# Attention with routed experts: row maxima are split into two parts before their transpose, and shift rows and running-sum rows travel in fewer DMAs

## The chip, the cores and the metric

One core of one Trainium2 chip runs the whole program in one launch. The metric is the device time of that launch in microseconds (us), lower is better. A median over three executions is given for the kernel before. One further execution was recorded by the hardware profiler; all rows below come from that one.

## What is computed

The first half is a causal attention for 8 batches of 8 heads, 576 positions of width 64, with a bias made from running sums of a gate `s`. The second half sends each of the 4,608 resulting tokens through a group router, an expert router and one of 16 two-layer experts.

```
scores = scale * q @ k^T                         # scale = 1/8
cum    = cumsum(max(s, 0), axis=-1)
bias   = -(cum[:, :, :, None] - cum[:, :, None, :])
scores = where(causal, -1e9, scores + minimum(bias, 0))
attn   = exp(scores - max(scores)); attn /= sum(attn) + 1e-9
x      = (attn @ v)  as 4608 rows of 512
g, e   = argmax of softmax(x @ w_group), then of softmax(x @ w_expert[g])
out    = p_g * p_e * (relu(x @ w1[g, e]) @ w2[g, e])
```

## The kernel before

The attention works head by head; two heads are a pair, so there are 32 pairs and four pairs to a batch. A loop over `step` from -4 to 68 handles one head in three roles at once: role A (`rowmax`) finds the row maxima of the head four steps ahead, role B (`scores`) makes the transposed scores of the current head and their exponentials, and role C (`av`) multiplies the previous head's probabilities by v.

*Maxima.* For A, TensorE multiplies 66 rows of the operand tile `WA` (64 of q or k, and rows 64 and 65, which carry the running sums in two parts) into the PSUM tile `pm` (L214). VectorE adds the causal mask and takes the maximum over each row into a column of `mc`, a tile of 128 partitions by 10 columns (five row blocks of each head of the pair, L222). After the pair's last maximum, `shift_rows` transposes `mc` on TensorE into the PSUM tile `pmt` (L236), ten rows of 128. `shifts` then writes the negated maxima as a high part `th` (L242) and the remainder `tl` (L243), both read from PSUM, and `send` issues two DMAs on ScalarE's queue (L248): `th` into row 66 of `WA`, `tl` into row 67. Every operand of the scores travels as such a high and a low part.

*Scores.* For B, TensorE multiplies all 68 rows of `WA` (L269) and adds the product of the low parts in `WB` (L271) in the PSUM tile `ps`. Rows 66 and 67 subtract the maximum, so the exponential on ScalarE (L279) needs no bias. GpSimd zeroes the masked triangle with affine_select (L288).

*The rest of a pair.* C writes the PSUM tile `po` (L309), ScalarE copies values and sums out (`vals` L313, `sums` L316), VectorE transposes the sums, takes reciprocals and multiplies (`st`, `rc`, `xT`, L335 to L354). q and k of a later pair are split by `split`: the high parts `hl` on ScalarE (L152), the low parts on GpSimd with a tensor_tensor of 576 columns (L156), from which `load_a` and `load_b` fill `WA` and `WB` by DMAs on SyncE's queue. `load_a` also fetches the running-sum rows 64 and 65 of `WA`, one DMA per head (L179), for pairs 0 to 3 from the SBUF tile `cumh` and later from its copy `cumd` in DRAM, which is written at the end of step -1 (L571). A `Router` works per batch in pieces between the attention's instructions; it needs a few constants, which `Router.operands` makes with eight VectorE instructions in one go at the end of step -1 (L668 to L678).

*What sets the order.* TensorE, VectorE, ScalarE and GpSimd follow an order written out by hand in strings. In the string of an even step, `... B3 T C1 A3 B1 ...` stands for score unit 3, then `T` (the transpose of the maxima), a piece of C, a piece of A, score unit 1; `t` makes the two parts, `D` sends, `R` lets the router go one piece on, `a` takes one maximum. SyncE's order is left to a scheduler after step 0. The tiles `ps`, `pmt` and the odd `px` share three PSUM buffers of one pool, and which one a tile gets follows from the readers that release them. All DMAs share eight completion semaphores.

Of the kernel before, what the change touches and what calls it, by code (L numbers as in the profile page):

```python
# [8 lines left out]
F32 = mybir.dt.float32  # L9
F32R = mybir.dt.float32r  # L10
# [3 lines left out]
ALU = mybir.AluOpType  # L14
# [6 lines left out]
P = 128  # L21
# [5 lines left out]
QO = 64  # L27
QW = QO + S
KA, QA = 0, 1
# [25 lines left out]
def attn_moe(ctx, tc, qk, v, s, wr, w1, w2, out, stop_at=None, dbg=None):  # L55
# [22 lines left out]
    st.listed = {}  # L78

    attention(tc, qk, v, s, wr, xs, st)  # L80
    if dbg is not None:
        nc.sync.dma_start(dbg['x'], xs)
# [26 lines left out]
def attention(tc, qk, v, s, wr, xs, st):  # L109
    nc = tc.nc  # L110
    NP = B * H // 2
    LEAD = 4
    with ExitStack() as ctx:
# [4 lines left out]
        sm = ctx.enter_context(tc.tile_pool(name="sm", bufs=2))  # L118
# [8 lines left out]
        ident = st.ident  # L127
# [5 lines left out]
        WA = [wa.tile([68, 2, 2, QW], F32R, name=f"WA{i}") for i in range(NA)]  # L133
# [13 lines left out]
        def split(p, part, later=False):  # L147

            if part == 0:
                hls[p] = raw.tile([P, 3, S], F32R, name=f"hl{p}", tag="hl", bufs=3)  # L150
            hl, r = hls[p], raws[p]
            nc.scalar.copy(hl[:, part], r[:, part])  # L152

            def low(h):
                hr = slice(0, P) if part else slice(h * 64, h * 64 + 64)
                (nc.vector if p < 1 else nc.gpsimd).tensor_tensor(  # L156
                    out=hl[:, 2] if part else WB[p % NBB][0:64, KA, h], in0=r[hr, part],
                    in1=hl[hr, part].bitcast(F32), op=ALU.subtract)

            for h in range(1 if part else 2):  # L160
                if later:
                    push("G", p, lambda h=h: low(h))
                else:
                    low(h)
# [7 lines left out]
        def load_a(p, placed=False):  # L172
            w = WA[p % NA]
            hl = hls[p].bitcast(F32)
            for h in range(2):
                if h or not placed:
                    nc.sync.dma_start(w[0:64, :, h, QO:].bitcast(F32), hl[h * 64:h * 64 + 64, 0:2])
                n = 2 * p + h
                nc.sync.dma_start(w[64:66, KA, h, QO:].bitcast(F32), (cumh if p < 4 else cumd)[n:n + 1].bitcast(F32))  # L179

        def load_b(p, placed=False):
            w = WB[p % NBB].bitcast(F32)
# [49 lines left out]
        def shift_rows(p):  # L232
            need("a", 2 * p + 1)
            i = p % NA
            pt = ring(f"pmt{p}", "t", True)
            nc.tensor.transpose(pt[:10, :P], mc[p % 2], ident)  # L236
            push("t", p, lambda: shifts(p, i, pt))

        def shifts(p, i, pt):
            th = sm.tile([10, P], F32R, name=f"th{p}", tag="th", bufs=1)  # L240
            tl = sm.tile([10, P], F32R, name=f"tl{p}", tag="tl", bufs=1)
            nc.vector.tensor_scalar(out=th, in0=pt[:10, :P], scalar1=-1.0, scalar2=None, op0=ALU.mult)  # L242
            nc.vector.scalar_tensor_tensor(out=tl, in0=pt[:10, :P], scalar=-1.0, in1=th.bitcast(F32), op0=ALU.mult,  # L243
                                           op1=ALU.subtract)

            def send():
                for r, t in ((66, th), (67, tl)):
                    nc.scalar.dma_start(WA[i][r:r + 1, QA].bitcast(F32).rearrange("o h q -> o (h q)"), t.bitcast(F32))  # L248

            push("D", p, send)  # L250

# [165 lines left out]
        def push(k, i, f):  # L417
            fifo[k].append((i, f))

        def pop(k):  # L420
            if fifo[k]:
                i, f = fifo[k].pop(0)
                done[k].append(i)
                f()
# [6 lines left out]
        def need(k, i):  # L431

            while fifo[k] and fifo[k][0][0] <= i:
                pop(k)

        def ring(name, k="b", reader=False):

            kind, n = ringed[-3]
            while n >= len(done[kind]):
                pop(kind)  # L440
            ringed.append((k, len(done[k]) + len(fifo[k]) if reader else -1))
            return ps_s.tile([P, 512], F32, name=name, tag="ps")
# [12 lines left out]
        cumh = c0[:BH, 0:2 * S].rearrange("p (a s) -> p a s", a=2)  # L455
        s0, r1, c2 = (c1[:BH, i * S:(i + 1) * S].bitcast(F32) for i in range(3))
        cumd = dr.tile([BH, 2, S], F32, name="cumd")
# [26 lines left out]
        mc = [ac.tile([P, 10], F32, name=f"mc{i}") for i in range(2)]  # L484
# [6 lines left out]
        split(0, 0)  # L491
        split(0, 1)
        load_a(0, True)
        split(1, 0)
        split(1, 1)
        load_raw(2)
        place(0, 1)
        place(0, 2)
        place(1, 0)
        load_a(1, True)  # L500
        load_b(0, True)
        rt = Router(tc, ac, late, end, kept, ring, wr_f, wr_sb, xs, st)
# [8 lines left out]
        for t in VT:  # L511
            nc.gpsimd.memset(t[:, 0:NB, 2], 1.0)


        pre = {-2: [(load_a, 2, True), (load_raw, 3), (load_v, 0)],
               -1: [(load_b, 1, True), (load_raw, 4)],
               0: [(split, 3, 0), (split, 3, 1), (load_a, 3), (load_v, 1)],
# [15 lines left out]
        for step in range(-LEAD, NH + 5):  # L533
            m, a = step + LEAD, step - 1
            A = rowmax(m) if m < NH else []
            Bq, C = [], []
            if 0 <= step < NH:
                need("T", step // 2)
                need("t", step // 2)
                need("D", step // 2)  # L540
                pts[step] = PT[step % 2]
                Bq = scores(step, pts[step])
            if 0 <= a < NH:
                p = a // 2
                for k in "be":
                    need(k, a)
                if a % 2 == 0:
                    for k in "YZWK":
                        need(k, p - 2)
                    vals[p] = sm.tile([P, S], F32, name=f"vals{p}", tag="vals", bufs=2)  # L550
                    sums[p] = sm.tile([P, S], F32, name=f"sums{p}", tag="sums", bufs=2)
                C = av(a, pts.pop(a), vals[p], sums[p])
            if step >= 2 and step // 2 + 4 < NP:
                push("S", step // 2 + 4, lambda p=step // 2 + 4, part=step % 2: split(p, part, True))
            named = {"A": A, "B": Bq, "C": C}
            order = FIRST if step < 3 else ORDERS if step < NH - 1 else LAST
            for part in order[step % 2] if step > 0 else ORDER0:
                if part[0] in named:
                    for f in named[part[0]][int(part[1]):int(part[1]) + 1]:
                        f()  # L560
                elif part == "R":
                    rt.step(rt.done >= B - 2)
                elif part == "J":
                    if rt.done >= B - 2:
                        rt.step(True)
                else:
                    pop(part)
            for f, *args in pre.get(step, ()):
                f(*args)
            if step == -1:  # L570
                nc.sync.dma_start(cumd, cumh.bitcast(F32))  # L571
                rt.operands()
            if step == 62:
                manual.close()
                manual.enter_context(tc.manual_schedule(engines={ENG.PE}))
            if step == 0:
                manual.close()
                manual.enter_context(tc.manual_schedule(engines={ENG.PE, ENG.DVE, ENG.Activation, ENG.Pool}))
            if step % 2 == 1 and 0 < step < NH:
                for f, lead in ((load_a, 4), (load_b, 3), (load_v, 1), (load_raw, 6)):  # L580
                    if step // 2 + lead < NP and (f != load_v or step > 1):
                        need("S", step // 2 + lead)
                        if f in (load_b, load_raw):
                            need("G", step // 2 + lead - 2 * (f == load_raw))
                        f(step // 2 + lead)
# [39 lines left out]
class Router:  # L625
# [39 lines left out]
        ni = ac.tile([P, B, NB], I32, name="ni")  # L665
        self.n1, self.ni, self.uf, self.onesf = n1, ni, uf, onesf

    def operands(self):  # L668
        V, ni, n1 = self.tc.nc.vector, self.ni, self.n1
        V.tensor_copy(self.wr_sb[:, :, 0:20], self.wr_f)  # L670
        V.tensor_tensor(out=self.wr_sb[:, :, 32:52], in0=self.wr_f, in1=self.wr_sb[:, :, 0:20].bitcast(F32),
                        op=ALU.subtract)
        V.tensor_copy(self.ub, self.uf)
        V.tensor_copy(self.ob, self.onesf)
        V.tensor_scalar(out=ni, in0=n1, scalar1=6, scalar2=None, op0=ALU.arith_shift_right)
        V.tensor_copy(self.part[:, 0], ni)
        V.tensor_scalar(out=ni, in0=n1, scalar1=63, scalar2=None, op0=ALU.bitwise_and)
        V.tensor_copy(self.part[:, 1], ni)  # L678

    def step(self, now=False):  # L680

# [906 lines left out]
```

## Time and profile before

| | us |
|---|---|
| median of three executions | 945.64 (940.46 to 947.15) |
| profiled execution | 939.42 |
| its span in the trace | 937.7 |
| attention with its routing, in that span | about 0 to 440 |
| experts | about 440 to 938 |

How the views are read: the page gives each engine's busy time and, in 40 slices, the busy tenths and the TensorE clock that was granted. The table by stretches gives the same per window. The wait table of TensorE lists which instruction it waited for, with the total, the count and the longest wait. A timeline gives start and duration of each instruction, and in square brackets the idle time of that engine just before it and what released it. "PEld" is TensorE's weight load, "ACTq" the issue of a DMA by ScalarE.

### The profile page before, as it was taken

What the parts mean: (1) busy time and instruction counts of PE and PEld (TensorE: products, weight loads), DVE (VectorE), ACT (ScalarE), POOL (GpSimd) and SP (SyncE); (2) the same over time, 40 slices, a digit from 0 to 9 for tenths busy, and PEclk for the clock granted to TensorE, in tenths of its full rate; (3) what the DMA queues carried; (4) which work ended last, traced back from release to release, by engine and by line L of the source; (5) the groups of instructions that cost most, each with busy time, mean ns of one, the idle gap of its engine ahead of it and who ended that gap; (6) DMA issues with size and microseconds to landing.
All of it is one profiled execution on the core that took longest, in us unless ns stands there. A gap on an engine that the chain in (4) does not pass through costs nothing. (4 is left out here: it accounts for less than half of the span.)

```text
span 937.7 us, 17973 instructions
## 1 busy us (share of the span) xinstructions
PE 867.3 (92%) x5648; PEld 779.6 (83%) x5648; DVE 702.2 (75%) x2002; ACT 608.3 (65%) x1382; POOL 615.0 (66%) x732
## 2 busy tenths in 40 slices
PE   4889999999999999998887999999999999999993
PEld 3677788888878787886686999999999999999992
DVE  7546685877868685876487578998888899888830
ACT  5567677776777677767734556667676666766740
POOL 9656576665757576534875447666768778878750
PEclk9989999999999999999998999999999999999997
DMA  6999989888989889723646345455554556655510
GB/s 188 237 209 228 213 218 227 198 223 188 226 204 223 215 210 231 175 68 114 207 139 210 134 162 192 165 190 208 184 194 180 204 185 226 226 201 188 195 44 23
DMA packets 80502, 174.66 MB, mean 186 GB/s; under 512 B 9580, under 2 KB 42988, under 8 KB 72208
## 3 DMA queue, kind: packets, MB, share of 16 engines
q1 hardware_dynamic: 70496, 153.52, 57.6%
q0 software_dynamic: 7488, 18.89, 5.7%
q10 hardware_dynamic: 2416, 1.03, 0.5%
q8 instruction: 47, 0.77, 0.4%
q14 instruction: 55, 0.45, 0.2%
HBM read 108.97 MB, written 19.69 MB: 137 GB/s over the span
## 5 line engine op out<-in xcount | busy, mean ns | idle before, releaser
L995 POOL TENSOR_TENSOR wl<-raw,wh 128x512 fp32r<-128x512 f32 x182 | 233.5, 1303 | 63.7 <-ACT wh L992 48.1
L222 DVE CUSTOM_DVE_ANT_0 mx<-pm,mask 128x192 bf16<-128x192 f32 (+4 forms) x320 | 129.3, 421 | 51.2 <-PE pm L214 47.5
L992 ACT CAST wh<-raw 128x512 fp32r<-128x512 f32 x256 | 153.8, 616 | 9.8 <-issue 9.2
L1093 PE MATMUL ph<-xl,wh 128*128 128x256 f32 (+13 forms) x512 | 145.0, 303 | 4.0 <-DVE xl L1065 3.6
L1093 PE MATMUL ph<-xh,wh 128*128 128x256 f32 (+13 forms) x512 | 144.1, 301 | 1.9 <-ACT xh L1064 1.1
L269 PE MATMUL ps<-WA 68*128 68x320 f32 (+4 forms) x384 | 136.0, 358 | 8.6 <-ACT pu L279 4.0
L214 PE MATMUL pm<-WA 66*128 66x288 f32 (+4 forms) x384 | 125.9, 356 | 18.4 <-DMA WA<-ch 10.4
L309 PE MATMUL po<-pt,VT 128*128 128x256 f32 (+3 forms) x512 | 122.2, 356 | 4.8 <-ACT sums L316 2.9
L1148 PE MATMUL py<-hl,wh 128*128 128x256 f32 (+13 forms) x448 | 112.7, 302 | 0.3 <-DVE hl L1089 0.3
L1148 PE MATMUL py<-hh,wh 128*128 128x256 f32 (+13 forms) x448 | 112.7, 301 | 0.0
L271 PE MATMUL ps<-WB 128*128 128x320 f32 (+4 forms) x384 | 110.2, 300 | 0.0
L1194 DVE STREAM_TRANSPOSE yr<-yT 32x384 f32<-32x384 f32 (+1 forms) x208 | 104.5, 502 | 4.3
L309 PE MATMUL po<-pu,VT 128*128 128x320 f32 (+1 forms) x384 | 106.3, 385 | 0.0
L1060 DVE STREAM_TRANSPOSE xt<-xg 32x256 f32<-32x256 f32 (+1 forms) x208 | 102.5, 493 | 3.2
L288 POOL TENSOR_SCALAR_AFFINE_SELECT pt<-pt 128x128 f32<-128x128 f32 (+2 forms) x192 | 65.0, 348 | 59.7 <-ACT pt L279 57.1
L309 PEld LDWEIGHTS po<-pt,VT 128*128 128x128 f32 x512 | 87.7, 192 | 18.4 <-issue 4.5
L1093 PEld LDWEIGHTS ph<-xl,wh 128*128 128x128 f32 x512 | 96.6, 189 | 7.3 <-DVE xl L1065 5.4
L1093 PEld LDWEIGHTS ph<-xh,wh 128*128 128x128 f32 x512 | 96.7, 189 | 3.9 <-ACT xh L1064 2.5
L1088 ACT ACTIVATE hh<-ph 128x256 fp32r<-128x256 f32 (+13 forms) x128 | 53.7, 420 | 66.4 <-PE ph L1093 65.7
L371 POOL TENSOR_TENSOR xTl<-xT,xTh 128x512 fp32r<-128x512 f32 x30 | 38.2, 1273 | 89.1 <-ACT xTh L367 81.6
L214 PEld LDWEIGHTS pm<-WA 66*128 66x128 f32 (+1 forms) x384 | 69.2, 192 | 32.0 <-DVE mc L222 15.3
L156 POOL TENSOR_TENSOR WB<-r,hl 64x576 fp32r<-64x576 f32 x62 | 87.2, 1406 | 5.3 <-DMA WB<-hl 2.4
(245 smaller groups left out, 2002.0 us busy)
## 6 DMA issues: line engine op xcount, KB each, us to landing
raw<-in_w_dram SPq DMA_DIRECT2D x64, 1024.0 KB
r<-in_qk_dram SPq DMA_DIRECT2D x32, 576.0 KB
WA<-hl SPq DMA_DIRECT2D x61, 288.0 KB
WB<-hl SPq DMA_DIRECT2D x61, 288.0 KB
VT<-in_v_dram SPq DMA_DIRECT2D x32, 384.0 KB
WB<-hl SPq DMA_DIRECT2D x64, 144.0 KB
xs<-xr SPq DMA_DIRECT2D x15, 512.0 KB
WA<-cumd SPq DMA_DIRECT2D x56, 4.5 KB
```

The costliest lines, as they stand in the source:

```text
L156: (nc.vector if p < 1 else nc.gpsimd).tensor_tensor(out=hl[:, 2] if part else WB[p % NBB][0:64, KA, h], in0=r[hr, part], in1=hl[hr, part]. ...
L214: nc.tensor.matmul(ps[:rows, :cw], WA[i][0:66, QA, h, QO + q0:QO + q0 + rows], WA[i][0:66, KA, h, QO + c0:QO + c0 + cw], start=True, stop= ...
L222: nc.vector.tensor_tensor_reduce(out=tmp[:rows, :cw], in0=ps[:rows, :cw], in1=mk[:rows], scale=1.0, scalar=-3.0e38 if c0 == 0 else mo, op0 ...
L269: nc.tensor.matmul(ps[:rows, o:o + w], WA[i][0:68, KA, h, QO + k0:QO + k0 + rows], WA[i][0:68, QA, h, QO + q0:QO + q0 + w], start=True, st ...
L271: nc.tensor.matmul(ps[:rows, o:o + w], WB[p % NBB][:, KA, h, k0:k0 + rows], WB[p % NBB][:, QA, h, q0:q0 + w], start=False, stop=True)
L309: nc.tensor.matmul(po[0][:, qa - base:qb - base], VT[p % NVT].rearrange("p t a d -> p (t a d)")[:, (3 * t + 1 + h) * 64:][:, 0:P], x[:, c: ...
L992: self.casts.append(nc.scalar.copy(h[:, j], raw[:, j]))
L995: self.low = nc.gpsimd.tensor_tensor(out=l[:, j], in0=raw[:, j], in1=h[:, j].bitcast(F32), op=ALU.subtract)
L1060: V.transpose(dst[:, 0:n, :, j], src[:, 0:n, :, i])
L1093: self.product = nc.tensor.matmul(pss[f][:, :cap], w[f // 4][:, c, (f % 4) * P:(f % 4 + 1) * P], x[:, c, :cap], start=(c == 0 and w is sel ...
L1148: self.product = nc.tensor.matmul(pss[c][:, :cap], w[2 + f // 4][:, f % 4, c * P:(c + 1) * P], x[:, f, :cap], start=(f == 0 and w is self. ...
L1194: V.transpose(dst[:, 0:n, :, i], src[:, 0:n, :, j])
```

## The change

Five edits, all in the attention:

1. `shift_rows` first makes the high and the low part of the negated maxima on VectorE, in the SBUF tile `mhl` (128 partitions by 2 times 10 columns), and TensorE transposes its 20 columns. `shifts` is one copy of 20 rows out of PSUM, and `send` is one DMA into rows 66 and 67. `th` has two buffers where it had one.
2. From pair 3 on, both heads' running-sum rows come in one DMA from `cumd`; pairs 0 to 2 read `cumh` as before.
3. `cumd` is written at the end of step -2, not -1.
4. `Router.operands` is cut in four pieces, made at the ends of steps 1 to 4.
5. At odd steps `load_v` is called ahead of `load_a` and `load_b`, not behind them.

```diff
@@ load_a
                 n = 2 * p + h
-                nc.sync.dma_start(w[64:66, KA, h, QO:].bitcast(F32), (cumh if p < 4 else cumd)[n:n + 1].bitcast(F32))
+                if p < 3:
+                    nc.sync.dma_start(w[64:66, KA, h, QO:].bitcast(F32), cumh[n:n + 1].bitcast(F32))
+            if p >= 3:
+                nc.sync.dma_start(w[64:66, KA, :, QO:].bitcast(F32),
+                                  cumd[2 * p:2 * p + 2].rearrange("h a s -> a h s"))
@@ shift_rows, shifts, send
+            m = sm.tile([P, 2, 10], F32R, name=f"mhl{p}", tag="mhl", bufs=2)
+            nc.vector.tensor_scalar(out=m[:, 0], in0=mc[p % 2], scalar1=-1.0, scalar2=None, op0=ALU.mult)
+            nc.vector.scalar_tensor_tensor(out=m[:, 1], in0=mc[p % 2], scalar=-1.0, in1=m[:, 0].bitcast(F32),
+                                           op0=ALU.mult, op1=ALU.subtract)
             pt = ring(f"pmt{p}", "t", True)
-            nc.tensor.transpose(pt[:10, :P], mc[p % 2], ident)
+            nc.tensor.transpose(pt[:20, :P], m.bitcast(F32).rearrange("p a n -> p (a n)"), ident)
...
-            th = sm.tile([10, P], F32R, name=f"th{p}", tag="th", bufs=1)
-            tl = sm.tile([10, P], F32R, name=f"tl{p}", tag="tl", bufs=1)
-            nc.vector.tensor_scalar(out=th, in0=pt[:10, :P], scalar1=-1.0, scalar2=None, op0=ALU.mult)
-            nc.vector.scalar_tensor_tensor(out=tl, in0=pt[:10, :P], scalar=-1.0, in1=th.bitcast(F32), op0=ALU.mult,
-                                           op1=ALU.subtract)
+            th = sm.tile([20, P], F32R, name=f"th{p}", tag="th", bufs=2)
+            nc.vector.tensor_copy(th, pt[:20, :P])
...
-                for r, t in ((66, th), (67, tl)):
-                    nc.scalar.dma_start(WA[i][r:r + 1, QA].bitcast(F32).rearrange("o h q -> o (h q)"), t.bitcast(F32))
+                nc.scalar.dma_start(WA[i][66:68, QA].bitcast(F32).rearrange("o h q -> o (h q)"), th.bitcast(F32))
@@ the loop over steps
-            if step == -1:
+            if step == -2:
                 nc.sync.dma_start(cumd, cumh.bitcast(F32))
-                rt.operands()
+            if 1 <= step < 5:
+                rt.operands(step - 1)
...
-                for f, lead in ((load_a, 4), (load_b, 3), (load_v, 1), (load_raw, 6)):
+                for f, lead in ((load_v, 1), (load_a, 4), (load_b, 3), (load_raw, 6)):
@@ Router.operands: the same eight instructions, two for each i of 0 to 3
```

The pairs of a batch follow a fixed pattern on the engines. They are named B, C, D and A here, in order of time, by the router's work around the transpose. On VectorE in a pair B, before (`col` and `rows` are the router's, `mc` the maxima):

```order
L222 ISA mx_4_0_2396,mc_153<-pm_4_0_2386,mask 128x288
L222 ISA mc_153 128x1
L848 TENSOR_TENSOR col_2398<-hot,pc_2337 128x320
L242 TENSOR_SCALAR th_2420<-pmt_2405 10x128
L243 SCALAR_TENSOR_TENSOR tl_2421<-pmt_2405,th_2420 10x128
L853 TENSOR_TENSOR rows_2424<-cols,pc_2337 128x640
```

And in the same place now:

```order
L226 ISA mx_4_0_2384,mc_153<-pm_4_0_2374,mask 128x288
L226 ISA mc_153 128x1
L855 TENSOR_TENSOR col_2386<-hot,pc_2326 128x320
L240 TENSOR_SCALAR mhl_2393<-mc_152 128x10
L241 SCALAR_TENSOR_TENSOR mhl_2393<-mc_152,mhl_2393 128x10
L249 CAST th_2411<-pmt_2396 20x128
L860 TENSOR_TENSOR rows_2413<-cols,pc_2326 128x640
```

The two parts stand behind the router's `col` and ahead of the transpose, which reads them; one copy stands behind it.

On VectorE in a pair C, before (`c` and `pi` are the router's token numbers in pieces):

```order
L222 ISA mc_152 128x1
L902 CAST c_2592<-pi_2521 128x5
L903 TENSOR_TENSOR pi_2521<-pi_2521,c_2592 128x5
L904 CAST c_2592<-pi_2521 128x5
L905 TENSOR_TENSOR c_2592<-pi_2521,c_2592 128x5
L242 TENSOR_SCALAR th_2618<-pmt_2603 10x128
L243 SCALAR_TENSOR_TENSOR tl_2619<-pmt_2603,th_2618 10x128
```

And now:

```order
L226 ISA mc_152 128x1
L909 CAST c_2579<-pi_2509 128x5
L910 TENSOR_TENSOR pi_2509<-pi_2509,c_2579 128x5
L911 CAST c_2579<-pi_2509 128x5
L912 TENSOR_TENSOR c_2579<-pi_2509,c_2579 128x5
L240 TENSOR_SCALAR mhl_2590<-mc_153 128x10
L241 SCALAR_TENSOR_TENSOR mhl_2590<-mc_153,mhl_2590 128x10
L249 CAST th_2608<-pmt_2593 20x128
```

Here the parts stand behind four of the router's instructions.

On TensorE in a pair A, with the engines whose semaphores an instruction waits for, before (`ps_0_256` is score unit 1):

```order
L236 MATMUL pmt_2979<-ident,mc_153 10x128 [waits Activation_49]
L309 MATMUL po_0_2968<-pu_120,VT_116 128x128
L214 MATMUL pm_2_0_2982<-WA_106 128x320
L269 MATMUL ps_0_256_2985<-WA_108 128x320 [waits Activation_49]
L271 MATMUL ps_0_256_2985<-WB_114 128x320
```

And now:

```order
L244 MATMUL pmt_2967<-ident,mhl_2964 20x128 [waits DVE_49,Activation_49]
L313 MATMUL po_0_2953<-pu_120,VT_116 128x128
L218 MATMUL pm_2_0_2970<-WA_106 128x320
L273 MATMUL ps_0_256_2973<-WA_108 128x320 [waits DVE_49]
L275 MATMUL ps_0_256_2973<-WB_114 128x320
```

TensorE's order is the same; the transpose has a new wait for VectorE, and score unit 1 waits for VectorE where it waited for ScalarE, because the three PSUM buffers are dealt out differently. In a pair C it is the other way round: there unit 1 waited for VectorE and now waits for ScalarE.

## Rows read from the trace of the kernel before

**Rows 1.** The page: busy time of TensorE and VectorE with the other engines, share of the span and instructions.

```profile
PE 867.3 (92%) x5648; PEld 779.6 (83%) x5648; DVE 702.2 (75%) x2002; ACT 608.3 (65%) x1382; POOL 615.0 (66%) x732
```

**Rows 2.** [...]

```profile
48.00:50.00 2.00, 2.00 (x8) 1.61 (x7) 1.05 (x5) 1.10 (x3) 1.93 (x4) 0.50 1.03 214
50.00:52.00 2.00, 2.00 (x10) 1.84 (x9) 0.55 (x3) 0.22 (x1) 0.64 (x3) 0.50 1.00 224
52.00:54.00 2.00, 2.00 (x7) 1.38 (x6) 0.27 (x2) 0.79 (x2) 0.00 (x0) 0.56 1.02 229
...
60.00:80.00 20.00, 17.02 (x106) 14.72 (x106) 11.63 (x44) 15.77 (x40) 11.24 (x17) 1.00 0.99 217
...
150.00:200.00 50.00, 48.33 (x307) 40.27 (x306) 37.93 (x148) 37.52 (x94) 31.87 (x50) 1.00 0.86 209
```

**Rows 3.** TensorE's waits between 100 and 400 us, nearly six batches: what waited for what, total us, times, longest.

```profile
PE pm L214 <- DVE mc L222: 3.9, 12, 0.4
PE ps L269 <- DVE tl L243: 3.0, 6, 0.5
PE ps L269 <- ACT pu L279: 2.0, 6, 0.3
```

**Rows 4.** The timeline of a pair B (start, us, engine, line, operation, tiles, shapes, count, idle time before and its releaser).

```profile
174.81 0.48 DVE L848 TENSOR_TENSOR col<-hot,pc 128x320 bf16<-128x320 bf16 x1
...
174.91 1.42 POOL L156 TENSOR_TENSOR WB<-r,hl 64x576 fp32r<-64x576 f32 x1
...
175.34 0.09 PEld L236 LDWEIGHTS pmt<-ident,mc 128*10 128x10 f32 x1
...
175.71 0.28 DVE L242 TENSOR_SCALAR th<-pmt 10x128 fp32r<-10x128 f32 x1 [0.42 <-PE pmt L236]
```

**Rows 5.** The timeline of a pair C.

```profile
187.14 1.41 POOL L156 TENSOR_TENSOR WB<-r,hl 64x576 fp32r<-64x576 f32 x1
...
187.56 0.09 PEld L236 LDWEIGHTS pmt<-ident,mc 128*10 128x10 f32 x1
...
187.64 0.17 DVE L903 TENSOR_TENSOR pi<-pi,c 128x5 f32<-128x5 f32 x1
...
188.05 0.17 DVE L905 TENSOR_TENSOR c<-pi,c 128x5 bf16<-128x5 f32 x1
188.13 0.28 DVE L242 TENSOR_SCALAR th<-pmt 10x128 fp32r<-10x128 f32 x1
...
188.44 0.54 ACT L279 ACTIVATE pu<-ps 128x448 f32<-128x448 f32 x1
...
188.78 0.42 PE L269 MATMUL ps<-WA 68*128 68x320 f32 x1 [0.50 <-DVE tl L243]
```

**Rows 6.** The timeline of a pair D.

```profile
199.22 0.08 DVE L222 DVE_READ_ACCUMULATOR2_ANT mc<- 128x1 f32 x1
199.23 0.29 POOL L288 TENSOR_SCALAR_AFFINE_SELECT pt<-pt 128x128 f32<-128x128 f32 x1 [0.40 <-ACT pt L279]
...
199.93 0.09 PEld L236 LDWEIGHTS pmt<-ident,mc 128*10 128x10 f32 x1
```

**Rows 7.** The timeline of a pair A.

```profile
213.87 0.09 PEld L236 LDWEIGHTS pmt<-ident,mc 128*10 128x10 f32 x1
...
214.23 0.28 DVE L242 TENSOR_SCALAR th<-pmt 10x128 fp32r<-10x128 f32 x1 [0.99 <-PE pmt L236]
214.30 0.55 ACT L279 ACTIVATE pu<-ps 128x448 f32<-128x448 f32 x1
...
214.90 0.41 PE L269 MATMUL ps<-WA 68*128 68x320 f32 x1 [0.34 <-ACT pu L279]
```

**Rows 8.** VectorE instructions with both inputs in SBUF, from three timelines: beside a GpSimd tensor_tensor, a small one and a large one, and the large one alone.

```profile
381.56 1.41 POOL L156 TENSOR_TENSOR hl<-r,hl 128x576 fp32r<-128x576 f32 x1
...
382.23 0.16 DVE L831 TENSOR_TENSOR count<-count,pc 128x16 f32<-128x16 f32 x1
...
190.13 1.40 POOL L156 TENSOR_TENSOR WB<-r,hl 64x576 fp32r<-64x576 f32 x1
...
191.02 1.13 DVE L354 TENSOR_TENSOR xT<-vals,st 128x576 f32<-128x576 f32 x1
...
219.06 0.76 DVE L354 TENSOR_TENSOR xT<-vals,st 128x576 f32<-128x576 f32 x1
```

**Rows 9.** The start. First TensorE's waits between 0 and 100 us, as in rows 3; then ScalarE's and TensorE's timeline around the sends of an early pair.

```profile
PE pm L214 <- DVE mc L222: 3.1, 5, 1.9
PE po L309 <- ACT sums L316: 2.9, 1, 2.9
PE ps L269 <- ACT pu L279: 1.9, 1, 1.9
PE ps L269 <- DMA WA<-tl: 1.6, 3, 0.9
...
59.94 0.75 ACTq L248 DMA_DIRECT2D WA<-th  x1
60.78 0.72 ACTq L248 DMA_DIRECT2D WA<-tl  x1
61.55 0.38 ACT L316 ACTIVATE sums<-po 64x256 f32<-64x256 f32 x1 [4.42 <-DMA WA<-th]
62.03 0.67 PE L309 MATMUL po<-pt,VT 128*128 128x256 f32 x2 [2.88 <-ACT sums L316]
```

More of the change, by code (lines that the diff above doesn't have):

```diff
@@ L666, in __init__, with operands @@
         self.n1, self.ni, self.uf, self.onesf = n1, ni, uf, onesf
-    def operands(self):
+    def operands(self, i):
         V, ni, n1 = self.tc.nc.vector, self.ni, self.n1
[L670 to L678, printed above, removed]
+        if i == 0:
+            V.tensor_copy(self.wr_sb[:, :, 0:20], self.wr_f)
+            V.tensor_tensor(out=self.wr_sb[:, :, 32:52], in0=self.wr_f, in1=self.wr_sb[:, :, 0:20].bitcast(F32),
+                            op=ALU.subtract)
+        elif i == 1:
+            V.tensor_copy(self.ub, self.uf)
+            V.tensor_copy(self.ob, self.onesf)
+        else:
+            op, by = ((ALU.arith_shift_right, 6), (ALU.bitwise_and, 63))[i - 2]
+            V.tensor_scalar(out=ni, in0=n1, scalar1=by, scalar2=None, op0=op)
+            V.tensor_copy(self.part[:, i - 2], ni)
     def step(self, now=False):
```

## The prediction

> **What bounds the kernel now.** I read the page's engine line first: TensorE is busy 867 of 937.7 us, VectorE 702 [rows 1]. A share is an average, so I went to the table by stretches. [...] So from about 100 us on, an edit counts by what it does to TensorE's waits, and 1.7 us idle in 50 is the most it could give back there; before 100 us it counts by what it does to ScalarE, VectorE and the DMA queues. The experts, from about 440 us, are not touched.
>
> The wait table of 100 to 400 us names those few waits. Three kinds hold 8.9 us, and two of them sit on score unit 1, right behind the transpose of the maxima: six waits of 0.50 for `tl` and six of about 0.33 for the exponential `pu` [rows 3]. The reader should see "x6" there: once per batch, so a place of the hand-written order, not chance. Six batches lie in that stretch; I count six, since the first pairs belong to the start and the last pairs have no pair four steps behind them. The timelines of the four pairs of a batch [rows 4 to 7] give the places: B, C, D, A.
>
> **The change, part by part.** The sum is made against the profiled execution, 939.42 us (span 937.7), which lies 6.2 us under the median 945.64; the result is carried to the median.
>
> *Maxima split before the transpose.* VectorE's work hardly changes: two reads of PSUM at 0.28 us become one such copy and two operations on 10 columns. What changes is the order of waiting: TensorE's transpose now waits for two small operations behind the last maximum, and everything behind the transpose on TensorE waits with it. Small dependent operations start 0.20 us apart (0.41 for two, from 187.64 to 188.05) and last 0.16 to 0.17 [rows 5].
> - D: the maximum starts at 199.22 and takes 0.08, the weight load of the transpose starts at 199.93 [rows 6]. The two parts are done by 199.30 + 0.20 + 0.16 = 199.66. Hidden by TensorE's other work, 0.27 us to spare: 0.
> - A: the same, VectorE is idle 0.99 us ahead of `th` [rows 7]. But score unit 1 there waited 0.34 us for the exponential `pu`, since it took the PSUM buffer that `pu` reads. In the new order's list it takes the buffer of the transpose and waits for VectorE instead. The copy starts where `th` did, 214.23, and ends at 214.51; TensorE came to unit 1 at 214.90 - 0.34 = 214.56. The wait goes: -0.33.
> - B: the router's `col`, 174.81 to 175.29, stands ahead. Parts at 175.29 and 175.49, done 175.65, weight load 0.03 behind it at 175.68 instead of 175.34 [rows 4]: +0.34.
> - C: four router instructions stand ahead, the last at 188.05; an independent one starts 0.08 behind it, as `th` did at 188.13. Parts at 188.13 and 188.33, done 188.49, weight load at 188.52 instead of 187.56: +0.96. TensorE stood 0.50 at unit 1 behind it for `tl`; now unit 1 waits for `pu`, which ends at 188.98, and TensorE comes there later than that (188.28 + 0.96 = 189.24) [rows 5]. So the old stall is swallowed: +0.46.
>
> A batch: -0.33 + 0.34 + 0.46 = +0.47, six of them **+2.8 us**. This rests on the small operations running as if alone while GpSimd works, because in B and C a GpSimd tensor_tensor of 1.4 us lies over them [rows 4, 5]. The nearest row says so: a 128x16 operation with both inputs in SBUF took 0.16 us in the middle of such a tensor_tensor. A large one did not: `xT` took 1.13 us beside one and 0.76 alone, and ended 0.62 behind GpSimd's end [rows 8]. The parts have 10 columns, so I take the small row.
>
> [...]
>
> Bounds of this part: below, B and C may be caught up at later waits of TensorE for maxima (3.9 us in all, rows 3), leaving -2.0; above, the first rival with both parts held, +15.3.
>
> *One send instead of two.* ScalarE issues one DMA less per pair, 0.72 us each and 0.8 with its pitch [rows 9]. In the settled stretch ScalarE has 12.5 of 50 us idle [rows 2] and no wait of TensorE names a shift row's DMA [rows 3]: 0. In the start it shows: ScalarE stood behind its own sends, so `sums` came late at 61.55 and TensorE waited 2.88; the second issue, 60.78 to 61.55, is 0.8 of that. And TensorE waited three times, 1.6 us, for `tl` to land [rows 9]; the high row, sent 0.8 earlier, caused none, so about 1.5 of it goes. **-2.3 us.** The long part, ScalarE held until the first send at 59.94 could go out, stays. Bounds: 0, if the one DMA takes as long as both; and the second rival.
>
> *Running sums, `cumd`, `load_v`.* Some 28 DMAs less on SyncE's queue and one issued a step sooner; `load_v` steps past the waits of `load_a` and `load_b`. No wait of TensorE in the settled stretch is for a DMA [rows 3], so SyncE's queue is covered by the lead of the loads: 0. If that cover were gone it would show as a wait for `WA` or `VT`. Should the scheduler hold a merged running-sum row back for both heads' buffers, a pair's first maximum could stand; bounded by the longest listed wait for a DMA, 0.9.
>
> *Constants in pieces.* One burst between maxima goes; TensorE's longest wait for a maximum in the start, 1.9 us, is of that kind [rows 9]. The pieces then stand between maxima of steps 1 to 4, where VectorE also feeds TensorE, and the first two transposes get the split's 0.4 to 0.9 each. I set gain against price: 0, with -1.9 and +1.9 as bounds.
>
> Sum: +2.8 - 2.3 + 0 = **+0.5 us**: 939.9 for the profiled execution, 946.1 on the median's footing.
>
> **Rivals.**
> 1. *The small operations are held by GpSimd (slower).* Then the second part, with its two SBUF inputs, ends about 0.1 behind GpSimd's end: in B at 176.33 + 0.12, weight load 176.48, +1.14; in C at 188.55 + 0.12, weight load 188.70, +1.14 less the swallowed 0.50. A batch: -0.33 + 1.14 + 0.64 = +1.45, six +8.7; with the start 6.4: 952.0. If the first part is held too, it loses the race in D against the tensor_tensor that begins as affine_select ends, at 199.52, and the transposes there move to about 201.0, 1.1 us late, six times +6.6: 958.6. For it: `xT`. Against: the 128x16 row. It decides from the point where the parts begin inside GpSimd's instruction.
> 2. *The start gives much more.* If fewer DMAs also free the completion semaphores that hold ScalarE's first send, then the waits for `sums` 2.9, `pu` 1.9, `tl` 1.6 and the maximum 1.9 all go, 8.3 instead of the 2.3 counted, and with them the stretch at the low clock (three windows of 2 us at 0.50, 0.50 and 0.56 lose 2.9 us against full clock): 946.1 - 6.0 - 2.9 = 937.2. For it: these waits stand close together. Against: the DMA engines are at 0.99 to 1.03 there [rows 2], and hardly a byte is saved.
> 3. *The start gives nothing*, as the queue and not the issue sets it: 946.1 + 2.3 = 948.4.
>
> **How the numbers follow.** The forecast has 0.50, rival 1 has 0.19 (0.13 at 952.0, 0.06 at 958.6), rival 2 0.15, rival 3 0.16. About 1% (9.5 us: under 936.2 or over 955.1) is what can be told from no change. The forecast's own range is 941 to 951. Faster by over 1% needs more than rival 2 gives at its middle: most of half of it and a little besides, 0.12. Slower by over 1%: the heavier half of rival 1 and the tail of the lighter one, 0.15. The rest, 0.73, within 1%. The range goes from 936.5, just under rival 2, to 955.5, which holds 952.0 with its spread and leaves out 958.6.
>
> **What would show it.** Right: between 100 and 400 us the six waits of unit 1 for `pu` and the six for `tl` are gone, the transpose has a wait for VectorE of about 0.35 in B and 0.95 in C and none in A and D, and TensorE's busy time per 50 us stays at 48.2 to 48.4; ScalarE's second send is gone at every pair and the wait at 62 us is under 2.3. Wrong: waits of the transpose of over 1.1 in B, or any in D (rival 1); no low clock around 50 us and under 10 us of waits before 100 us (rival 2); unchanged waits there (rival 3); new waits for `WA` or `VT` (the loads).

## The result, and the profile after

The changed kernel takes 952.58 us (median of 21 runs) against 945.86 for the kernel before on the same chips: a ratio of 1.0070, 95% interval 1.0047 to 1.0094, or +6.6 us (+4.4 to +8.9). The forecast was 946.1 with a range of 936.5 to 955.5; the result lies inside the range and near the 952.0 of rival 1, not at the forecast. The profiled execution of the kernel before is a short one (939.42 against a median of 945.86), that of the changed kernel a usual one (953.57), so their spans of 937.7 and 951.8 are not compared; single rows are, place by place.

TensorE's waits after, between 100 and 400 us, in the columns of [rows 3]:

```profile
PE pmt L244 <- DVE mhl L241: 12.7, 11, 1.2
PE pm L218 <- DVE mc L226: 3.9, 12, 0.4
```

The two waits of score unit 1 (3.0 and 2.0 us) are gone, as the new dealing of PSUM buffers led to expect. In their place TensorE waits at the transpose, eleven times 1.15 us, in B and in C, not 0.35 and 0.95. A pair B of the changed kernel, VectorE, GpSimd and TensorE, to be laid beside [rows 4]:

```profile
235.75 0.48 DVE L855 TENSOR_TENSOR col<-hot,pc 128x320 bf16<-128x320 bf16 x1
235.86 1.40 POOL L156 TENSOR_TENSOR WB<-r,hl 64x576 fp32r<-64x576 f32 x1
...
236.15 1.14 DVE L240 TENSOR_SCALAR mhl<-mc 128x10 fp32r<-128x10 f32 x1
...
237.32 0.20 DVE L241 SCALAR_TENSOR_TENSOR mhl<-mc,mhl 128x10 fp32r<-128x10 f32 x1
...
237.67 0.27 PE L244 MATMUL pmt<-ident,mhl 128*20 128x128 f32 x1 [1.16 <-DVE mhl L241]
```

Ten columns take 1.14 us: the first part starts 0.29 us into GpSimd's instruction and ends at 237.29, 0.03 behind that instruction's end at 237.26. It is held. A pair C shows which operations are, and which are not, beside the same GpSimd instruction:

```profile
248.78 1.41 POOL L156 TENSOR_TENSOR WB<-r,hl 64x576 fp32r<-64x576 f32 x1
...
249.28 0.17 DVE L910 TENSOR_TENSOR pi<-pi,c 128x5 f32<-128x5 f32 x1
249.49 0.17 DVE L911 CAST c<-pi 128x5 bf16<-128x5 f32 x1
249.69 0.17 DVE L912 TENSOR_TENSOR c<-pi,c 128x5 bf16<-128x5 f32 x1
249.77 0.46 DVE L240 TENSOR_SCALAR mhl<-mc 128x10 fp32r<-128x10 f32 x1
...
250.57 0.27 PE L244 MATMUL pmt<-ident,mhl 128*20 128x128 f32 x1 [1.14 <-DVE mhl L241]
```

Three of the router's operations run at 0.17 us inside it, and the part behind them stands until its end. In pairs D and A of the settled stretch the parts take 0.17 us and the transpose does not wait. The difference between the two groups is where their inputs lie: `pi` is a PSUM tile, which TensorE's matmuls write, and `mc` lies in SBUF. The runs under "What is held" come back to this.

The start is the second place. TensorE's waits before 100 us, in the columns of [rows 9]:

```profile
PE ps L273 <- DMA WA<-th: 6.9, 4, 2.8
PE pmt L244 <- DVE mhl L241: 3.7, 3, 1.8
PE po L313 <- issue: 2.1, 1, 2.1
PE pm L218 <- DVE mc L226: 1.8, 5, 0.6
```

The longest of the waits for the send, in the timeline:

```profile
98.01 0.55 PE L273 MATMUL ps<-WA 68*128 68x256 f32 x1 [2.81 <-DMA WA<-th]
```

The 1.9 for a maximum is gone. The 2.9 for `sums` only changed its name: ScalarE still stands behind its send, and TensorE waits 2.08 at the same place, which the list puts down to "issue":

```profile
62.07 0.64 ACTq L252 DMA_DIRECT2D WA<-th  x1
62.76 0.38 ACT L320 ACTIVATE sums<-po 64x256 f32<-64x256 f32 x1 [3.67 <-DVE mc L226]
63.24 0.67 PE L313 MATMUL po<-pt,VT 128*128 128x256 f32 x2 [2.08 <-issue]
```

The 3.7 for `mhl` are the first three transposes, 0.95, 0.86 and 1.85. The waits for the shift rows have grown from 1.6 to 6.9 us, and around the last and longest one the clock falls, to 0.85 and 0.81 of full speed in the stretches below, where the kernel before was granted 1.00. The table by stretches after, in the columns of [rows 2]: the stretch, its length, busy us (and instructions) of TensorE, its weight load, VectorE, ScalarE and GpSimd, the granted TensorE clock as a share of full speed, the DMA engines' busy share, GB/s.

```profile
80.00:90.00 10.00, 7.54 (x46) 6.26 (x45) 5.17 (x21) 6.33 (x16) 7.05 (x12) 1.00 1.10 232
90.00:100.00 10.00, 7.19 (x42) 6.16 (x41) 4.65 (x20) 6.06 (x17) 4.38 (x8) 0.85 1.07 183
100.00:110.00 10.00, 10.00 (x54) 9.03 (x53) 7.33 (x22) 6.17 (x15) 4.08 (x6) 0.81 0.88 203
```

Why would one DMA land later than two? The page's line of the queue that carries the sends (packets, MB, share), of the kernel before and then of the changed one:

```profile
q10 hardware_dynamic: 2416, 1.03, 0.5%
```

```profile
q10 hardware_dynamic: 1840, 1.02, 0.4%
```

576 packets fewer. Counted by size in the two traces, the 640 packets of 512 bytes, the rows themselves, are the same; those of 4 bytes go from 688 to 112. With 64 sends before and 32 after that is ten per send and two per send, and 48 others. So a send of ten rows had ten packets of 4 bytes with it before, and a send of twenty rows has two now, while the DMA engines are full (share 1.07 to 1.10 above, between 80 and 100 us). The author took this to mean that two DMA engines serve the single send where ten served each of the two; no trace names the engine of a packet, so it is not shown. That the rows are late by coming one behind the other does not show either. For the four sends issued between 60 and 105 us the first row's packet comes 4.8 to 6.4 us after the issue, against 3.0 to 3.5 before, and all twenty are through 1.3 to 2.6 us after it; before, the ten of `tl` alone took 2.3 to 2.7. The lateness lies ahead of the first row, and why is not shown.

### The profile page after: what moved, and what is told of

It reads as the page before. It is cut to its first block, busy times and chain, and to the rows that moved or that the text cites. A ratio compares the mean times of both kernels' runs of the same rounds, so it can differ in the third digit from the quotient of the medians.

```text
span 951.8 us, 17885 instructions
## 1 busy us (share of the span) xinstructions
PE 869.2 (91%) x5648; PEld 784.8 (82%) x5648; DVE 710.7 (75%) x2034; ACT 609.6 (64%) x1382; POOL 614.6 (65%) x732
## 5 line engine op out<-in xcount | busy, mean ns | idle before, releaser
L999 ACT CAST wh<-raw 128x512 fp32r<-128x512 f32 x256 | 154.1, 617 | 10.2 <-issue 9.5
L292 POOL TENSOR_SCALAR_AFFINE_SELECT pt<-pt 128x128 f32<-128x128 f32 (+2 forms) x192 | 67.4, 362 | 62.2 <-ACT pt L283 59.9
```

The costliest lines, as they stand in the source:

```text
L999: self.casts.append(nc.scalar.copy(h[:, j], raw[:, j]))
```

## The experiments

Two theories stood after the traces. *Hold*: VectorE's first part is held by GpSimd's tensor_tensor, and TensorE pays in B and C. *Engines*: the single send is served by two DMA engines, which is the author's supposition from the packets of 4 bytes, and lands late in the full start. Their rival was that the other edits (constants, order of loads, running sums) or chance make the loss. Ratios below are to the kernel before on the same chip, with 95% intervals.

**Two sends.** In the changed kernel:

```diff
-                nc.scalar.dma_start(WA[i][66:68, QA]..., th.bitcast(F32))
+                for r in range(2):
+                    nc.scalar.dma_start(WA[i][66 + r:67 + r, QA]..., th[10 * r:10 * r + 10].bitcast(F32))
```

> The changed kernel with its one send cut back into two DMAs of ten rows each. Theory (the send's ten rows per DMA row are served one behind the other by two DMA engines, while the two DMAs before had ten engines each): the queue of the sends writes about 10 completion words per DMA again, the first sends land some 1 to 2 us sooner, TensorE's waits for WA<-th before 100 us fall from 6.9 to under 3, and the time is 3 to 5 us under the changed kernel's, at about 948 to 949. Rival (the start is lost to the constants in pieces, the order of the loads or chance): the waits stay or move to sums, and the time is that of the changed kernel or 1 to 2 us above it, 952 to 955. By both, the waits of the transpose between 100 and 400 us stay at 12 to 13 us.

949.27 us, 1.0027 (1.0003 to 1.0050). The queue's line is that of the kernel before again (2416 packets), and the waits before 100 us for `th` are 3.1 us, not 6.9:

```profile
PE ps L275 <- DMA WA<-th: 3.1, 2, 2.2
```

About 4 us of the loss come back (1.0070 to 1.0027), and the waits for `mhl` stay at 12.6. Between 60 and 105 us the sends have landed 6.9 us after the first issue on average, 0.8 sooner than the single one and not 1 to 2. The intervals of the two ratios just overlap; a second pair of runs below gives the same difference. The waits for `th` of one trace are weak evidence, for they scatter: 1.0 to 6.9 us in the six traces with one send, 0.7 to 5.6 in the seven with two (for `tl` where there are two tiles). The landings overlap as well, with means per trace of 5.9 to 8.4 and 6.2 to 8.0. So the run shows that two sends cost less than one. It does not show that the number of engines is the reason: a single DMA with its ten row blocks outermost, meant to tell the engines from the number of DMAs, was not measured.

**Only the other edits.** The kernel before with the running sums, `cumd`, the constants and the order of loads as changed, and maxima, transpose and two sends as they were.

> The kernel before with the running sums in one DMA, cumd a step sooner, constants in pieces and load_v first, and maxima, transpose and two sends as before. Theory (all loss comes from the split ahead of the transpose and from the single send): no more than 1 us from before, 945 to 946.5, with no new waits in the start. Rival (these edits cost the start): 948 or more, with waits for maxima or for WA before 100 us.

945.18 us, 0.9982 (0.9956 to 1.0007). These four edits cost nothing that can be measured. In its trace the wait of 1.9 for a maximum is gone, the gain that the prediction had named for the constants, and one wait of 3.1 us for `cumd` stands in the start, which the kernel before lacks; the prediction had allowed 0.9 for that. The wait behind ScalarE's sends is 1.97 here, with two sends, and 2.08 in the changed kernel, with one.

**A later transpose.** `T` moved back in even steps:

```diff
-  ... e G a R a B3 T C1 A3 B1 A2 C2 b e t R C3 v G C4 ...
+  ... e G a R a B3 C1 A3 B1 A2 C2 b e T R C3 t v G C4 ...
```

> The changed kernel with the transpose of the maxima (and the two parts ahead of it) moved back in the order of even steps, from behind score unit 3 to behind the exponentials of unit 1, so that the parts start after GpSimd's tensor_tensor. Theory (GpSimd's tensor_tensor holds the small operations, and TensorE pays for it six times in B and C): the parts take 0.17 us each everywhere, TensorE's waits for mhl between 100 and 400 us fall from 12.7 to under 3 us, and the time is 4 to 6 us under the changed kernel: 947 to 948.5. Rival (TensorE's loss in the settled stretch has another source, such as the new dealing of PSUM buffers): the waits for mhl go, but others of like size stand in their place and the time stays within 2 us of 952.6.

959.65 us, 1.0111 (1.0076 to 1.0146): slower, where a gain of 5 was expected. The thought was wrong at its first step. VectorE reaches the parts as soon as the maxima are done, wherever the transpose stands on TensorE, and finds GpSimd busy as before. Its timeline in a pair B, and then its waits of 100 to 400 us:

```profile
133.75 1.15 DVE L240 TENSOR_SCALAR mhl<-mc 128x10 fp32r<-128x10 f32 x1
```

```profile
PE pm L218 <- DVE mc L226: 10.2, 28, 0.5
```

No wait for the parts is left, but now TensorE waits for maxima, 10.2 us instead of 3.9. That the held VectorE reaches TensorE by this way is not shown: a run below has the same waits with nothing held. The start lost as well, with 3.6 us for `pt` and 3.8 for `th`.

**GpSimd's tensor_tensor later.** In even steps of the changed kernel the first `G` goes behind the affine_select of `pu`, the second to the end of the step; no instruction of VectorE or TensorE moves.

```diff
-  ... C0 e G a R a B3 T C1 A3 B1 A2 C2 b e t R C3 v G C4 ... C5 e C6 b a A5
+  ... C0 e a R a B3 T C1 A3 B1 A2 C2 b e G t R C3 v C4 ... C5 e C6 G b a A5
```

> The changed kernel with GpSimd's two low-part tensor_tensors of even steps moved later in the order: the first from ahead of the transpose to behind the affine_select of pu, the second to the end of the step. The parts keep their place and now find GpSimd idle. Theory (GpSimd's tensor_tensor holds VectorE's first part, and that is the loss of the settled stretch): each part takes 0.17 us, TensorE's waits for mhl between 100 and 400 us fall from 12.7 to about 5 us (0.35 in B, 0.5 in C), and the pairs between 120 and 430 us come at the pace of before, 0 to 0.5 us later per batch instead of 0.9: 3 to 5 us under the changed kernel, 948 to 949.5. Rival (the order of the parts behind the router's work is what costs): waits for mhl and the pace stay, 952 to 953. If GpSimd's affine_selects are pushed late, TensorE would wait for pt instead; then neither number holds.

948.91 us, 1.0023 (0.9994 to 1.0053). Its timeline in a pair B, and its waits of 100 to 400 us:

```profile
231.06 0.17 DVE L240 TENSOR_SCALAR mhl<-mc 128x10 fp32r<-128x10 f32 x1
231.26 0.17 DVE L241 SCALAR_TENSOR_TENSOR mhl<-mc,mhl 128x10 fp32r<-128x10 f32 x1
...
231.80 1.42 POOL L156 TENSOR_TENSOR WB<-r,hl 64x576 fp32r<-64x576 f32 x1
```

```profile
PE pm L218 <- DVE mc L226: 6.4, 18, 0.4
PE pmt L244 <- DVE mhl L241: 4.3, 5, 0.9
```

With GpSimd out of the way the parts take 0.17 each, and the transpose waits long in C alone, five times 0.9, where the working for unheld parts had 0.96; the 0.35 it had for B does not show. The pace, from the start of `xT` of pair 11 to that of pair 27, four batches: 52.31 us per batch before, 53.14 in the changed kernel, 52.82 here. Theory Hold stands, against the rival that the parts' place behind the router's work is what costs. The 0.5 that is left against the kernel before needs the next run.

The same move in the kernel before, as a control:

> The kernel before with GpSimd's two tensor_tensors of even steps moved later, as was done to the changed kernel. Theory (the move helped there only by freeing the parts): no gain here, 945 to 947.5, waits of the settled stretch as before (3.9 for maxima, 3.0 for tl, 2.0 for pu). Rival (the move is a gain of its own for any kernel): 941 to 943.5, and the changed kernel's loss is not shown to be the hold.

948.88 us, 1.0027 (0.9996 to 1.0058). It gains nothing there; a cost of some 2 us is inside the interval, but the waits for maxima grow as they did in the changed kernel (5.8 instead of 3.9). So the gain in the changed kernel is not one of the move. A batch that the clock left alone, from `xT` of pair 11 to that of pair 15, tells more; first the changed kernel with the move, then the kernel before with it:

```profile
205.78 1.78 DVE L358 TENSOR_TENSOR xT<-vals,st 128x576 f32<-128x576 f32 x1
258.60 1.78 DVE L358 TENSOR_TENSOR xT<-vals,st 128x576 f32<-128x576 f32 x1
```

```profile
204.31 1.75 DVE L354 TENSOR_TENSOR xT<-vals,st 128x576 f32<-128x576 f32 x1
257.12 1.76 DVE L354 TENSOR_TENSOR xT<-vals,st 128x576 f32<-128x576 f32 x1
```

| pair 11 to pair 15, us | GpSimd as it was | GpSimd later |
|---|---|---|
| kernel before | 52.33 | 52.81 |
| changed kernel | 53.22 | 52.82 |

The move itself costs 0.5 us per batch in the kernel before, where this `xT` takes 1.75 instead of 0.76. With the move both kernels keep one pace, so parts that are not held cost nothing per batch. With GpSimd as it was they cost 0.83 per batch (53.14 less 52.31), 5.0 us for six. By this pace the hold is the whole loss of the settled stretch, and its price is more than the difference of the two runs.

**Both.** The changed kernel with two sends and GpSimd's tensor_tensors later.

> The changed kernel with GpSimd's two tensor_tensors moved as in the run before and the send cut into two DMAs of ten rows. Theory (hold and single send are the two causes, and they add): the gain of both, 3 to 5 and 3.3 us under the changed kernel, 944.5 to 946.5, level with the kernel before. Rival (they share one cause): no better than the better of the two.

944.36 us, 0.9987 (0.9954 to 1.0020): level with the kernel before. The four ratios make a square:

| | one send | two sends |
|---|---|---|
| parts held | 1.0070 | 1.0027 |
| parts not held | 1.0023 | 0.9987 |

Moving GpSimd's work gains 0.0047 and 0.0040, the second send 0.0043 and 0.0036. Averaged, that is 0.0043 and 0.0040, each within 0.0028 if the four intervals are taken as independent: two causes of about 4 us each, both clear of nothing. Whether they just add is known only to 0.0055. In the settled stretch this run is still 0.48 us per batch slower than the kernel before (52.80), the price of the move; where it makes that up was not followed.

With the later transpose on top, from step 8 on:

> As the run before, and from step 8 on the transpose stands behind the exponentials of unit 1 in even steps. Theory (with the parts unheld and TensorE past its place before they end, nothing waits, and the old waits of score unit 1, 5 us between 100 and 400, are gone too): no waits for mhl, 2 to 4 us under the run before and under the kernel before, 941 to 944. Rival (as with the later transpose alone, the loss turns into waits for maxima, since VectorE and not the place of the transpose bounds): equal to the run before or slower, 945 to 950.

951.96 us, 1.0062 (1.0030 to 1.0094): the rival, and slower than its 950. No wait for the parts, but 9.4 us for maxima in 100 to 400. Moving the transpose costs by itself; why the maxima come later when nothing holds VectorE was not followed up.

**What is held.** Four runs asked which kind of small operation GpSimd's tensor_tensor holds. Three plain tensor_tensors instead of the two kinds used:

> The changed kernel, the parts made by three plain tensor_tensors of two SBUF inputs (zero minus mc, mc plus the high part, zero minus that) instead of a tensor_scalar and a scalar_tensor_tensor. [...]

959.07 us, 1.0133 (1.0087 to 1.0179). On record before it ran were 949 to 951, if none of the three is held, and 953 to 955 with 14 to 16 us of waits, if the first is. The first is, though the time is above 955 and the transpose waits 12.5 us for `mhl` and 6.7 for `pu`, more than the 16. The first of the three is held as the tensor_scalar was, here in a pair B, and in pairs D the third is, which begins 0.1 us inside the next GpSimd instruction and takes 1.3:

```profile
129.34 1.13 DVE L241 TENSOR_TENSOR mhl<-zero,mc 128x10 fp32r<-128x10 f32 x1
130.50 0.20 DVE L242 TENSOR_TENSOR mt<-mc,mhl 128x10 f32<-128x10 f32 x1
130.74 0.17 DVE L243 TENSOR_TENSOR mhl<-zero,mt 128x10 fp32r<-128x10 f32 x1
```

The parts interleaved, written to every second element (with two sends):

> The changed kernel with two sends, the two parts interleaved in their tile (column by column, high and low side by side), so that the parts write every second element instead of ten in a row; the rows of the transpose interleave too and each send takes every second one. Theory (GpSimd's tensor_tensor holds only operations whose operands all lie element behind element, as xT and the parts do and the router's small unheld operations beside the same GpSimd instruction do not): parts 0.17 us in B and C, waits for mhl between 100 and 400 us 4 to 5 us instead of 12.6, 945 to 947. Rival (any two-input or copying operation with its inputs in SBUF): waits stay at 12 to 13, 949 to 950, as with two sends alone.

946.48 us, 1.0010 (0.9982 to 1.0038), but the waits for `mhl` are 12.6 as in the run with two sends, and the first part takes 1.14: held all the same. This is a second run with parts held and two sends: 1.0010 here, 1.0027 above, which differ within their intervals.

An operation in place, and one with a broadcast operand:

> The changed kernel, the parts made by three operations: the maxima negated in place, a copy as the high part, a tensor_tensor as the low part. Looked at for the durations alone. Theory (an operation that writes over its own input, as the router's unheld ones do, is let through inside GpSimd's tensor_tensor): in B the in-place one takes 0.17 us and the next one is held, about 0.9 us. Rival (what is held is not told by that): the first one takes 1.14 us, the others 0.17 to 0.2.

> As the run with three tensor_tensors, the zero operand of the first and the third now read as one element repeated over five columns (a broadcast), as the router's plt<-plt,lmx reads its second operand. That router operation began inside the same GpSimd instruction and took its usual 0.27 us. Looked at for the durations alone. Theory (a broadcast operand lets an operation through): in B the first one takes about 0.17 us where it took 1.13. Rival (what lets the router's operations through is something else): 1.13 again.

Both were run for the durations; their times are single executions, 960.93 and 958.42 us, with 951.44 and 945.02 for the kernel before beside them. The first operation of each in a pair B:

```profile
126.24 1.14 DVE L240 TENSOR_SCALAR mc<-mc 128x10 f32<-128x10 f32 x1
```

```profile
125.03 1.13 DVE L241 TENSOR_TENSOR mhl<-zero,mc 128x10 fp32r<-128x10 f32 x1
```

Held again. So neither the operation, nor the stride of its output, nor writing in place, nor a broadcast decides. What all four runs left as it was is where the inputs lie: the parts read SBUF alone. The operations of the router that the expectations took as their measure read an input from PSUM, since `pc`, `pi`, `plt` and `pw` are tiles of the kernel's PSUM pool `ps_t`. The kernel before shows it on the parts themselves. They read `pmt` from PSUM there; `th` of [rows 4] begins 0.80 us inside GpSimd's instruction and takes its usual 0.28, and so does `tl` behind it, also inside:

```profile
176.03 0.28 DVE L243 SCALAR_TENSOR_TENSOR tl<-pmt,th 10x128 fp32r<-10x128 f32 x1
```

In that trace 27 `th` and 26 `tl` begin inside a GpSimd tensor_tensor, and none takes longer than 0.28. In the trace of the changed kernel, the operations that are held there (the parts, up to 1.34 us against 0.17; `xT`, up to 1.78 against 0.76; `xl<-xt,xh` of the experts, up to 1.34 against 0.69 to 0.88) read SBUF alone, and none with an input in PSUM is held: the copy of `pmt` takes 0.28 inside and outside, all 32 times. Not all that read SBUF alone are held: the reciprocal `rc` takes 0.26 to 0.27 us inside and outside. So, by all that the traces show, the change laid the two operations open to GpSimd by taking them from a PSUM input to SBUF inputs. No run tried the parts ahead of the transpose with an input in PSUM.

## Why the prediction was right and wrong

*Right by its range, wrong in its likeliest case.* The range held the time because rival 1 and rival 3 were in it.

- The step that failed first: "a 128x16 operation with both inputs in SBUF took 0.16 us in the middle of such a tensor_tensor", and with it "I take the small row." The row was misread. `pc` in `count<-count,pc` is a PSUM tile, so the operation has one input in SBUF, and the heading of [rows 8] is wrong for it. `xT`, whose inputs both lie in SBUF, was the row to go by, far larger as it is. The parts were held, the first of them and not the second as rival 1 had it.
- The size of the settled part: 0.83 us per batch against 0.47 forecast and 1.45 in rival 1 (53.14 less 52.31). Held, B and C do not cost the full sum, since TensorE makes up part of it in D and A: between the `xT` of consecutive pairs the changed kernel loses 1.0 in B and about 0.3 in C against the kernel before, and gains 0.2 in D and 0.3 in A. Unheld it is 0.0 and not the 0.47 of the sum, if each kernel has GpSimd's work later: -0.3 in A, 0.0 in B, +0.4 in C and -0.15 in D. So A (-0.33) and C (+0.46) were sized right; the +0.34 of B and the nothing of D were not.
- That the time came out beside the 952.0 of rival 1 is luck: its sum has +8.7 in the settled stretch and -2.3 in the start, where the settled stretch shows +5.0, which leaves some 1.6 for the rest.
- The second step that failed: "the one DMA takes as long as both" was the worst that the single send was allowed. The bound was too narrow. The single send lands 7.7 us after its issue on average between 60 and 105 us, both of the two 6.8 after the first, and costs some 4 us by the square, where -2.3 was forecast. That fewer DMA engines share it is the author's supposition from the packets of 4 bytes, two per send instead of ten; no run shows it. The 0.8 of it that was to come from ScalarE's saved issue does not show: the wait is 2.08 with one send and 1.97 with two.
- Right: the waits of score unit 1 went, by the buffers that the new order named; transposes in D and A do not wait from 100 us on; constants, running sums, `cumd` and `load_v` together come to nothing (0.9982, 0.9956 to 1.0007). From `xT` of the last pair to the end it took 483.9 us before and 485.8 after, inside the 482.4 to 486.8 of all traces, so a change in the experts does not show.
- Rival 2 was wrong: fewer DMAs freed nothing in the full start, and the clock fell all the same, to 0.54 of full speed between 40 and 50 us in the changed kernel, 0.50 from 40 to 48, and once more between 90 and 110, to 0.85 and 0.81. Whether the waits bring it on no run shows.

## What to carry to other kernels

A small VectorE operation, put on TensorE's path, was priced here by where its inputs lie and by what GpSimd does at that moment: 0.28 us from PSUM beside a GpSimd tensor_tensor, up to 1.34 from SBUF. Before a row is taken as the measure of another operation, look up in the kernel which memory each of its tiles is in; a trace line does not say. Merging two DMAs into one saved an issue (0.72 us), but in the start, with the DMA engines full (share 1.07 to 1.10 between 80 and 100 us), the merged one landed later, 7.7 us after its issue against 6.8 after the first of two; why is not shown. When instructions are moved to test a cause, run the same move in the kernel before: here the move had a price of its own. And when a stall is moved off one wait of TensorE, look at the others: here waits for maxima came up.

## What the runs showed that was not expected

A 128x10 operation of the parts on VectorE, with its inputs in SBUF, takes 0.17 us alone and up to 1.34 beside a GpSimd tensor_tensor of 64x576 (1.41 us), ending 0.03 behind it, while operations on five columns with an input in PSUM take 0.17 inside the same instruction. One 20-row send had all its rows landed 6.6 to 8.8 us after its issue between 60 and 105 us; two ten-row sends of the kernel before, 6.3 to 7.9 after the first issue there and 5.4 to 7.1 after the second. And single executions of one kernel differ by what the clock does: in the run with only the other edits, 270 to 280 us was granted 0.83 of full speed, and the pairs behind it came 1.7 us later at once:

```profile
270.00:280.00 10.00, 9.35 (x56) 7.75 (x56) 7.79 (x35) 6.04 (x16) 3.41 (x7) 0.83 0.47 114
280.00:290.00 10.00, 9.85 (x59) 8.44 (x59) 8.97 (x33) 7.20 (x17) 7.18 (x12) 1.00 0.83 198
```
